# Seven products instead of eight in part of the first MLP, and a new order behind the attention

## The chip, the cores and the metric

The kernel runs as one program on one core of a Trainium2 chip. The core has five engines that take their instructions in order, each from its own queue: TensorE (PE in the profile, with its weight loads shown apart as PEld), VectorE (DVE), ScalarE (ACT), GpSimd (POOL) and SyncE (SP, which here only issues DMAs). They wait for each other through semaphores. The metric is the device time of one execution in microseconds, as the median over runs. Before the change it is 654.48 us (three runs, 653.82 to 654.96).

## The reference

Three stages, each feeding the next, in float32:

```
out_d     = attention of q, k, v averaged over groups of 4 positions, repeated 4 times
out_local = attention within |i - j| < 4
x   = (out_d + out_local), as 1152 tokens x 512                 # 2 batches of 576
h   = x @ w_in                                                  # 512 -> 2048
x   = where(h > 0, h, exp(min(h, 0)) - 1) @ w_out              # 2048 -> 512, "first MLP"
for e in 4 experts:                                             # "second MLP"
    out += p[:, e] * (relu(x @ w1[e]) @ w2[e])                  # 512 -> 1024 -> 512
```

`p` is `domain_probs` with its rows normalized. `w_in` and `w_out` come as 64-bit floats, of which the kernel makes 32-bit ones itself.

## The kernel before

**Number form.** TensorE works on a 32-bit type with a shorter mantissa. Every operand X is therefore split into a high part (a copy into that type, on ACT) and a low part (X minus the high part, on DVE or POOL), and every product is three matmuls: high x high, low x high, high x low (`PASSES`, `mm3`, L237 to L242). All matmuls that the change touches have a 128x128 stationary operand and 288 moving columns.

**Stages.** The attention of batch 0 and 1 runs first (`Attn`). The first MLP cuts its 2048 features into four quarters s = 0 to 3 of 512 and the 1152 tokens into four blocks t = 0 to 3 of 288 (t = 0, 1 are batch 0, t = 2, 3 batch 1). In a quarter, f = 0 to 3 counts blocks of 128 features, mt = 0 to 3 blocks of 128 output columns. The second MLP (from L1023) runs over eight pieces of 512 features; in it the first product already stands in seven-product form (`quad`, L1075), and its first piece, n = 0, uses weights prepared during the first MLP.

**Steps.** The work up to the second MLP is one long string `ORDER` (L23), read from left to right; a step is named by its letters and its indices, and ":v" or ":g" puts it on DVE or POOL. Each engine runs its own steps in the order of this string. The steps that matter here:

- `hp.s.t.f` (PE, L788): x times one block of `w_in`, four stretches of 128 inputs, so 12 matmuls into one of eight PSUM banks. `yp.s.t.mt` (PE, L829): features times `w_out`, again 12 matmuls.
- `ha`, `he` (ACT), `hd` (DVE): the activation; `hh` (ACT) and `hl` (DVE or POOL): high and low part `g` of its result; `ya` (DVE, for s = 0 ACT): adds the bank of `yp` to the accumulator.
- `wF` (DMA), `wA` (ACT), `wB` to `wE` (DVE, L274, L280, L287, L294), `wH` (ACT) and `wL` (DVE or POOL, L308): fetch of a 64-bit weight piece, conversion to 32 bits, high and low part.
- `xh`, `xl`, `xd`, `xth`, `xtl`: high and low parts, and differences, of the accumulators, as inputs of the second MLP's first product.
- `mF`, `mS`, `mH`, `mL`, `nF`, `nH`, `nL`: weights of piece n = 0 of the second MLP: fetch, sums (POOL, L348), high parts (ACT), low parts (POOL, L376, L400).
- `C`: the attention's memory is given up, and pools that take its place are opened (L931 to L937).

Behind `C` stand 41 `hp` and 46 `yp`. Tiles live in slots (`Slots`, L121): one that is given back goes to the end of a list, and the next tile waits, through semaphores, for the last reader of the tile before it in its slot. In the second MLP the same kind of steps is started from a list of due times (`due`, `plan`, L1293 to L1348); after the first MLP, `xd` and then `first_xt` (L1336) for the second half of the tokens come from there, on POOL.

## Time and profile before

| | us |
|---|---|
| median of 3 runs | 654.48 |
| the profiled execution's own time | 654.35 |
| its span, first to last instruction | 652.6 |
| PE busy | 645.2 |
| DVE / ACT / POOL busy | 450.7 / 302.2 / 316.9 |
| behind `C` up to the second MLP, 139.31 to 277.91 us: length | 138.60 |
| there: PE / DVE / ACT / POOL busy | 138.60 / 96.70 / 80.66 / 53.94 |

The span is what the profiler saw of the core; 1.75 us of the execution lie around it. Busy times are unions of an engine's instructions, so instructions that overlap are counted once, and an instruction held up after its start by something that the profile doesn't show as a wait is still counted as busy. A wait is shown as idle time ahead of an instruction, with what ended it.

### The profile page before, as it was taken

Reading aid. Unit: us, or ns where it says so; the run is one execution under the profiler, and the core shown is the slowest. Engines: PE = TensorE matmul, PEld = TensorE weight load, DVE = VectorE, ACT = ScalarE, POOL = GpSimd, SP = SyncE. Lnnn points to the kernel's source line nnn. Section 1 sums busy time; section 2 is a strip of 40 time slices with the busy share of each in tenths; the row PEclk is TensorE's granted clock in tenths of the full one; section 3 lists DMA queues with packets and bytes.
Section 4 is the critical chain, followed back from the end, with each engine's and each line's share of the span. In section 5 each row is a group of like instructions: output and inputs, shape, how many; then the busy total and the mean of one; then the engine's idle time right before and its main releaser. Section 6 shows DMA issues by size and latency. Waiting matters only on the chain.

```text
span 652.6 us, 12355 instructions
## 1 busy us (share of the span) xinstructions
PE 645.2 (99%) x4804; PEld 593.0 (91%) x4804; DVE 450.7 (69%) x957; ACT 302.2 (46%) x825; POOL 316.9 (49%) x312
## 2 busy tenths in 40 slices
...
GB/s 240 211 200 224 166 87 11 1 196 66 65 130 65 130 2 1 2 65 1 66 65 1 112 18 7 124 0 66 66 2 64 66 1 67 62 1 66 1 48 97
DMA packets 40880, 46.70 MB, mean 72 GB/s; under 512 B 23030, under 2 KB 23286, under 8 KB 40822
## 3 DMA queue, kind: packets, MB, share of 16 engines
...
q14 instruction: 20, 0.16, 0.1%
...
## 4 chain that ended last, share of the span: by engine, by line
PE 91%; DVE 4%; DMA 3%; issue 1%; ACT 0%; SPq 0%; DVEq 0%
PE psZ L240 30%; PE psH L240 17%; PE psY L240 14%; PE psE L240 7%; PE psA L240 6%; PE psG L240 3%; PE psF L240 3%; PE psB L240 2%; PE psS L585 1%; PE psX L645 1%; DMA raw<-in_k_dram 1%; DMA raw<-in_moe_w_in_dram 1%; PE psP L629 1%; PE psC L240 1%; PE psGT L736 1%; PE psG L682 1%
## 5 line engine op out<-in xcount | busy, mean ns | idle before, releaser
L240 PE MATMUL psZ<-wr,h 128*128 128x512 f32 (+2 forms) x876 | 226.8, 390 | 0.0
L240 PEld LDWEIGHTS psZ<-wr,h 128*128 128x128 f32 x876 | 154.4, 188 | 22.1
L240 PE MATMUL psH<-x,w 128*128 128x288 f32 x768 | 108.0, 296 | 1.7 <-DVE w L308 1.4
L240 PE MATMUL psY<-g,w 128*128 128x288 f32 x768 | 106.3, 296 | 0.1
L240 PEld LDWEIGHTS psH<-x,w 128*128 128x128 f32 x768 | 103.3, 188 | 3.3 <-DVE w L308 2.2
L240 PEld LDWEIGHTS psY<-g,w 128*128 128x128 f32 x768 | 103.3, 188 | 0.5 <-DVE g L826 0.3
L1138 DVE SCALAR_TENSOR_TENSOR oacc<-psZ,pn,oacc 128x512 f32<-128x512 f32 (+1 forms) x64 | 47.4, 740 | 45.1 <-PE psZ L240 45.1
L1043 ACT ACTIVATE h<-psF 128x288 fp32r<-128x288 f32 x28 | 11.5, 412 | 118.2 <-DVE psF L1037 118.2
L826 POOL TENSOR_TENSOR g<-gf,g 128x288 fp32r<-128x288 f32 x25 | 22.0, 883 | 80.6 <-ACT g L821 78.0
L240 PEld LDWEIGHTS psE<-xt,ws 128*128 128x128 f32 x336 | 48.6, 188 | 3.3
L240 PE MATMUL psE<-xt,ws 128*128 128x288 f32 x336 | 50.6, 295 | 0.0
L1000 POOL TENSOR_TENSOR wq<-raw,wq 128x512 fp32r<-128x512 f32 x21 | 27.0, 1301 | 47.1 <-ACT wq L996 42.9
L400 POOL TENSOR_TENSOR wr<-raw,wr 128x1024 fp32r<-128x1024 f32 x16 | 38.6, 2419 | 21.0 <-ACT wr L395 20.9
L1037 DVE TENSOR_TENSOR c<-psE,c 128x288 f32<-128x288 f32 x56 | 25.4, 456 | 33.7 <-PE psE L240 33.4
L1010 POOL TENSOR_TENSOR raw<-raw 128x256 f32<-128x256 f32 x56 | 42.6, 766 | 3.4
L821 ACT ACTIVATE g<-gf 128x288 fp32r<-128x288 f32 x64 | 27.3, 440 | 28.2 <-DVE gf L814 21.3
L814 DVE SCALAR_TENSOR_TENSOR gf<-m,psH 128x288 f32<-128x288 f32 x64 | 28.0, 446 | 16.7 <-ACT m L809 11.9
L1037 DVE TENSOR_TENSOR c<-psA,c 128x288 f32<-128x288 f32 x62 | 26.6, 454 | 17.8 <-PE psA L240 16.6
L395 ACT ACTIVATE wr<-raw 128x1024 fp32r<-128x1024 f32 x16 | 16.8, 1058 | 43.1 <-DMA raw<-in_moe_w_dram 22.7
L1018 POOL TENSOR_TENSOR ws<-raw,ws 128x1024 fp32r<-128x1024 f32 x14 | 34.1, 2457 | 2.5 <-ACT ws L1014 2.5
L805 ACT ACTIVATE m<-psH 128x288 f32<-128x288 f32 x64 | 25.3, 402 | 19.4 <-PE psH L240 14.9
L308 POOL TENSOR_TENSOR w<-raw,w 128x512 fp32r<-128x512 f32 x12 | 18.6, 1550 | 30.2 <-ACT w L303 30.2
...
## 6 DMA issues: line engine op xcount, KB each, us to landing
...
```

The costliest lines, as they stand in the source:

```text
L240: nc.tensor.matmul(ps, wt[a], xt[b], start=first and n == 0, stop=last and n == 2, skip_group_check=more)
L308: ENG[eng].tensor_tensor(out=t[:, 1, r], in0=up.bitcast(F32), in1=t[:, 0, r].bitcast(F32), op=ALU.subtract)
L400: nc.gpsimd.tensor_tensor(out=t[:, 1], in0=raw[0][:, 2 * j:2 * j + 2], in1=t[:, 0].bitcast(F32), op=ALU.subtract)
L805: nc.scalar.activation(m, ps1["h", s, t, f][:, :HB], AF.Relu, scale=-1.0)
L814: nc.vector.scalar_tensor_tensor(out=gf, in0=m, scalar=-1.0, in1=ps[:, :HB], op0=ALU.add, op1=ALU.max)
L821: nc.scalar.activation(g[:, 0], ps1["gf", s, t, f], AF.Copy)
L826: ENG[eng].tensor_tensor(out=g[:, 1], in0=gf, in1=g[:, 0].bitcast(F32), op=ALU.subtract)
L1000: tt(out=lo, in0=x, in1=hi.bitcast(F32), op=sub)
L1010: tt(out=o, in0=a, in1=b, op=op)
L1018: tt(out=w[:, 1], in0=raw[0][:, :, 2 * j * P:2 * (j + 1) * P], in1=w[:, 0].bitcast(F32), op=sub)
L1037: nc.vector.tensor_tensor(out=o, in0=y, in1=x, op=add_)
L1138: nc.vector.scalar_tensor_tensor(out=a, in0=ps, scalar=sc, in1=a, op0=ALU.mult, op1=ALU.add)
```

## The change

For the last quarter (s = 3), the four `hp` steps that share a pair of feature blocks (j = 0 or 1) and a batch (b = 0 or 1) form a 2x2 block product, over two halves of the inputs: eight block products, each 2x3 matmuls. In three of the four such groups (`QUADS`) they are replaced by seven products `qp.s.j.b.k`, of sums and differences of the blocks. The fourth group, (3, 1, 1), keeps its four `hp`. For this:

- `xa` (eight steps a batch, DVE or POOL, 128x576) forms four sums of x, `xi` (ACT) and `xj` (DVE or POOL) their high and low parts. They live in new tiles, for batch 0 in memory that is given back at a new step `D`.
- `vS` (four steps a j, DVE) forms sums of the converted weights in place, `vH` (ACT) and `vL` (DVE or POOL) their high and low parts, in two new tiles.
- `qc` (three steps a group, ACT) copies one PSUM bank at three points, and `qd` (five steps a group, DVE) adds the pieces; products 3 and 6 accumulate into the bank of product 0.
- The pool of three large tiles becomes three pools of one.
- All of `ORDER` behind `C` is written anew: 533 steps before, 615 now. Steps common to both stand in another order and partly on another engine. Up to `C` nothing differs.

```diff
 ORDER = """
...
-1LPh.6 ha.1.2.3 1LPl.6:v yp.0.2.0 C wF.2.1:b ya.0.2.0 ya.0.2.1 hh.1.2.0 wF.2.0:b wA.2.0 he.1.2.3 wA.2.1 hl.1.2.0:v
...
+1LPh.6 ha.1.2.3 1LPl.6:v yp.0.2.0 C hp.0.3.2 ya.1.1.3 he.1.2.3 wF.2.0:b xa.0.0:g wF.2.1:b hh.1.2.0 ya.1.0.2 hh.1.2.1
...
-    xp = ctx.enter_context(tc.tile_pool(name="xp", bufs=3))
+    xp = [ctx.enter_context(tc.tile_pool(name=f"xp{i}", bufs=1)) for i in range(3)]
...
+        def quarters(p):
+            a, b = (piece(2 * p + i)[2].bitcast(F32) for i in range(2))
+            return a[:, :, :P], a[:, :, P:], b[:, :, :P], b[:, :, P:]
+        def vS(p, o, eng="g"):
+            f0a, f1a, f0b, f1b = quarters(p)
+            out, x, y, op = (
+                (f1b, f1a, f1b, ALU.add), (f1a, f0a, f1a, ALU.subtract), (f0a, f1b, f0a, ALU.subtract),
+                (f0b, f0b, f0a, ALU.subtract),
+            )[o]
+            ENG[eng].tensor_tensor(out=out, in0=x, in1=y, op=op)
+        def vH(p, i):
+            shape, r, up, _ = piece(2 * p + i)
+            if i == 0:
+                wv[p] = s8.tile([P, 2, *shape], F32R, name="v64", uses=sums[p])
+            nc.scalar.activation(wv[p][:, 0, r], up.bitcast(F32), AF.Copy)
+        def vL(p, i, eng="g"):
+            _, r, up, _ = piece(2 * p + i)
+            ENG[eng].tensor_tensor(
+                out=wv[p][:, 1, r], in0=up.bitcast(F32), in1=wv[p][:, 0, r].bitcast(F32), op=ALU.subtract
+            )
+            where[p].done(raw[p])
...
+        QUADS = {(3, 0, 0), (3, 1, 0), (3, 0, 1)}
+        def quads(s, j):
+            return sum((s, j, b) in QUADS for b in range(2))
...
+        def xa(b, k, eng="g"):
+            if k == 0:
+                xs[b] = (xp[2] if b else bo[0]).tile([P, 4, 2, 2, HB], F32R, tag="x" if b else "xs", name="xs")
+                x32[b] = bo[1].tile([P, 4, 2, HB], F32, tag="x32", name="x32")
+            o = [x32[b][:, n] for n in range(4)]
+            def x(h, i):
+                return [xb[b][:, m, 2 * h:2 * h + 2, i * HB:(i + 1) * HB].bitcast(F32) for m in range(2)]
+            out, x, y, op = (
+                (o[0], *x(0, 0), ALU.add), (o[1], *x(0, 1), ALU.add), (o[0], o[1], o[0], ALU.subtract),
+                (o[2], *x(1, 1), ALU.add), (o[1], o[2], o[1], ALU.subtract), (o[2], o[2], o[0], ALU.subtract),
+                (o[3], *x(1, 0), ALU.add), (o[3], o[3], o[2], ALU.subtract),
+            )[k]
+            ENG[eng].tensor_tensor(out=out, in0=x, in1=y, op=op)
+        def xi(b, n):
+            nc.scalar.activation(xs[b][:, n, 0], x32[b][:, n], AF.Copy)
+        def xj(b, n, eng="g"):
+            x = xs[b][:, n]
+            ENG[eng].tensor_tensor(out=x[:, 1], in0=x32[b][:, n], in1=x[:, 0].bitcast(F32), op=ALU.subtract)
+        def qp(s, j, b, k):
+            w, v = wt[s][0][j], wv[s][j]
+            def wb(w, h, i):
+                return [w[:, m, 2 * h:2 * h + 2, i * P:(i + 1) * P] for m in range(2)]
+            def xv(h, i):
+                return [xb[b][:, m, 2 * h:2 * h + 2, i * HB:(i + 1) * HB] for m in range(2)]
+            def xn(n):
+                return [xs[b][:, n, m] for m in range(2)]
+            (wh, wl), (h, l) = (
+                lambda: (wb(w, 0, 0), xv(0, 0)), lambda: (wb(w, 1, 0), xv(1, 0)), lambda: (wb(v, 1, 1), xn(0)),
+                lambda: (wb(v, 0, 0), xn(2)), lambda: (wb(v, 1, 0), xv(1, 1)), lambda: (wb(w, 1, 1), xn(3)),
+                lambda: (wb(v, 0, 1), xn(1)),
+            )[k]()
+            if k == 0:
+                if not ct:
+                    c = st_pool[0].tile([P, 4, 2, P], F32, tag="st", name="ct").rearrange("p a b c -> p (a b c)")
+                    ct.extend(c[:, i * HB:(i + 1) * HB] for i in range(3))
+                ps1["q", s, j, b] = [ct]
+            q = ps1["q", s, j, b]
+            if k in (3, 6):
+                q.append(None)
+            else:
+                q.append(bank("psQ"))
+            ps = q[1 if k in (3, 6) else k + 1][:, :HB]
+            for kk in range(2):
+                mm3(ps, (wh[:, kk], wl[:, kk]), (h[:, kk], l[:, kk]), k not in (3, 6) and kk == 0, kk == 1, k in (3, 6))
+            if k == 5:
+                s8.done(w)
+            if k == 6:
+                s8.done(v)
+        def qc(s, j, b, n):
+            q = ps1["q", s, j, b]
+            nc.scalar.activation(q[0][n], q[1][:, :HB], AF.Copy)
+            if n == 2:
+                psb_.done(q[1])
+        def qd(s, j, b, n):
+            q = ps1["q", s, j, b]
+            c1, u2, u3 = q[0]
+            ps = q[(2, 3, 5, 6, 3)[n]]
+            y = ps[:, :HB]
+            nc.vector.tensor_tensor(
+                out=u2 if n == 1 else y, in0=y, in1=(c1, u2, u2, u3, u3)[n], op=ALU.add
+            )
+            if n != 1:
+                i, k = {0: (0, 0), 2: (0, 1), 3: (1, 0), 4: (1, 1)}[n]
+                ps1["h", s, 2 * b + k, 2 * j + i] = ps
...
-                xto[pair] = xp.tile([P, 4, 2, 2, HB], F32R, tag="x", name="xt")
+                xto[pair] = xp[1 - pair].tile([P, 4, 2, 2, HB], F32R, tag="x", name="xt")
...
+                bo.extend(xst.enter_context(tc.tile_pool(name=x, bufs=1)) for x in ("xs", "x32"))
...
+            if tok == "D":
+                xst.close()
+                bo[:] = [ctx.enter_context(tc.tile_pool(name="bo", bufs=2))]
+                continue
...
-        oacc = xp.tile([P, NTT, DM], F32, tag="x", name="oacc")
+        oacc = xp[2].tile([P, NTT, DM], F32, tag="x", name="oacc")```

**VectorE just behind `C`.** `g` is a low part (`hl`), `acc` an accumulation (`ya`), `gf` the activation (`hd`), `xf` the attention's last work, `cv` and `raw` the conversion of weights. Before:

```order
227 L656 TENSOR_TENSOR xf<-psX,od 128x256
228 L670 TENSOR_TENSOR x_831<-xf,x_831 128x4x64
229 L826 TENSOR_TENSOR g<-gf,g 128x288
230 L274 TENSOR_SCALAR cv<-cv 128x512
231 L280 TENSOR_SCALAR cv<-cv 128x512
232 L274 TENSOR_SCALAR cv<-cv 128x512
233 L287 SCALAR_TENSOR_TENSOR raw_2624<-raw_2624,cv 128x512
```

Now, where the 128x576 rows are `xa` and the last row is the low part `hl.1.2.2`, which the ninth PE step behind `C` (`yp.1.2.0`) reads:

```order
232 L855 TENSOR_TENSOR x_2644<-x_326 128x576
233 L941 TENSOR_TENSOR g<-gf,g 128x288
234 L929 SCALAR_TENSOR_TENSOR gf<-m,psH 128x288 x2
235 L941 TENSOR_TENSOR g<-gf,g 128x288
236 L855 TENSOR_TENSOR x_2644<-x_326 128x576
237 L855 TENSOR_TENSOR x_2644<-x_2644 128x576 x2
238 L929 SCALAR_TENSOR_TENSOR gf<-m,psH 128x288
239 L281 TENSOR_SCALAR cv<-cv 128x512 x2
240 L287 TENSOR_SCALAR cv<-cv 128x512 x2
241 L294 SCALAR_TENSOR_TENSOR raw_2641<-raw_2641,cv 128x512 x2
242 L301 SCALAR_TENSOR_TENSOR raw_2641<-raw_2641 128x512 x2
243 L941 TENSOR_TENSOR g<-gf,g 128x288
```

The weight conversion moved behind the activations and four new sums, and one low part, on POOL before, stands behind all of it.

**TensorE in the last quarter.** `psQ` are the products of the new form, `x_326` and `x_837` the two batches, `xs` their sums, `v` the sums of weights:

```order
296 L247 MATMUL psQ<-x_326,w_3405 128x288 x12
297 L247 MATMUL psQ<-xs,v_3470 128x288 x12
298 L247 MATMUL psQ<-x_326,v_3470 128x288 x6
299 L247 MATMUL psQ<-xs,w_3405 128x288 x6
300 L247 MATMUL psQ<-xs,v_3470 128x288 x6
```

This is one group: seven products in 42 matmuls where four `hp` had 48. There are three such groups, and 18 matmuls fewer.

**POOL at the passage to the second MLP.** `ws` and `wr` are low parts of weights of piece n = 0, `st` sums of them, `xbo` and the first `xt` rows low parts of the first half, `acc` and the last `xt` row the second half (`xd`, `first_xt`). Before:

```order
82 L376 TENSOR_TENSOR ws<-st,ws 128x4x256
83 L826 TENSOR_TENSOR g<-gf,g 128x288 x2
84 L871 TENSOR_TENSOR xbo<-acc,xbo 128x288 x2
85 L826 TENSOR_TENSOR g<-gf,g 128x288
86 L890 TENSOR_TENSOR xt<-acc,xt 128x576
87 L871 TENSOR_TENSOR xbo<-acc,xbo 128x288
88 L880 TENSOR_TENSOR acc<-acc 128x576 x3
89 L890 TENSOR_TENSOR xt<-acc,xt 128x576 x4
```

Now:

```order
94 L380 TENSOR_TENSOR st<-raw_3936,st 128x256
95 L986 TENSOR_TENSOR xbo<-acc,xbo 128x288
96 L408 TENSOR_TENSOR ws<-st,ws 128x4x256
97 L432 TENSOR_TENSOR wr<-raw_4054,wr 128x1024
98 L995 TENSOR_TENSOR acc<-acc 128x576 x3
99 L1005 TENSOR_TENSOR xt<-acc,xt 128x576 x4
```

The last `ws` and `wr` moved to the very end, between the last low part of the first MLP and the differences that the second MLP's third group reads.

## Rows read from the trace of the kernel before

**Rows 1.** The page's busy times: us, share of the span, instructions.
```profile
PE 645.2 (99%) x4804; PEld 593.0 (91%) x4804; DVE 450.7 (69%) x957; ACT 302.2 (46%) x825; POOL 316.9 (49%) x312
```

**Rows 2.** Windows: length; PE, PEld, DVE, ACT, POOL busy; clock; DMA; GB/s.
```profile
40.00:80.00 40.00, 38.58 (x452) 35.55 (x448) 39.58 (x76) 33.61 (x108) 19.11 (x18) 1.00 0.99 208
80.00:120.00 40.00, 39.19 (x415) 37.29 (x414) 37.10 (x86) 30.89 (x116) 12.51 (x14) 1.00 0.16 43
200.00:240.00 40.00, 40.00 (x304) 40.00 (x304) 32.95 (x56) 20.86 (x49) 16.73 (x16) 1.00 0.23 80
139.31:277.91 138.60, 138.60 (x1046) 138.60 (x1045) 96.70 (x188) 80.66 (x189) 53.94 (x50) 1.00 0.18 62
```

**Rows 3.** Timeline of TensorE: start, us, line, out<-in, count.
```profile
139.31 3.35 PE L240 MATMUL psH<-x,w 128*128 128x288 f32 x24
...
277.91 1.76 PE L240 MATMUL psH<-xbo,wa 128*128 128x288 f32 x12
...
289.11 1.76 PE L240 MATMUL psH<-xbo,wa 128*128 128x288 f32 x12
...
293.91 0.96 PE L240 MATMUL psH<-xt,ws 128*128 128x288 f32 x6
```

**Rows 4.** VectorE groups, 160 to 278 us: xcount | busy us, mean ns | idle.
```profile
L854 DVE TENSOR_TENSOR acc<-psY,acc 128x288 f32<-128x288 f32 x36 | 15.4, 449 | 10.1 <-PE psY L240 10.1
L826 DVE TENSOR_TENSOR g<-gf,g 128x288 fp32r<-128x288 f32 x20 | 12.9, 648 | 2.8 <-ACT g L821 2.7
L294 DVE SCALAR_TENSOR_TENSOR raw<-raw 128x512 uint32<-128x512 uint32 x12 | 9.6, 796 | 0.2
...
L274 DVE TENSOR_SCALAR cv<-cv 128x512 f32<-128x512 f32 x12 | 7.6, 636 | 6.7 <-ACT cv L270 6.7
...
L880 DVE TENSOR_TENSOR acc<-acc 128x576 f32<-128x576 f32 x4 | 3.0, 750 | 0.0
```

**Rows 5.** Timeline of VectorE, single instructions.
```profile
137.35 0.42 DVE L670 TENSOR_TENSOR x<-xf,x 128x256 fp32r<-128x256 f32 x1 [0.48 <-ACT x L665]
...
141.72 0.43 DVE L280 TENSOR_SCALAR cv<-cv 128x512 uint32<-128x512 uint32 x1
...
144.29 0.69 DVE L294 SCALAR_TENSOR_TENSOR raw<-raw 128x512 uint32<-128x512 uint32 x1
...
275.36 0.75 DVE L890 TENSOR_TENSOR xt<-acc,xt 128x576 fp32r<-128x576 f32 x1
...
279.44 1.36 DVE L890 TENSOR_TENSOR xt<-acc,xt 128x576 fp32r<-128x576 f32 x1
```

**Rows 6.** Timeline of GpSimd at the passage to the second MLP.
```profile
279.08 1.11 POOL L871 TENSOR_TENSOR xbo<-acc,xbo 128x288 fp32r<-128x288 f32 x1
281.92 4.47 POOL L880 TENSOR_TENSOR acc<-acc 128x576 f32<-128x576 f32 x3 [1.73 <-DVE acc L880]
...
287.97 4.22 POOL L890 TENSOR_TENSOR xt<-acc,xt 128x576 fp32r<-128x576 f32 x3 [0.19 <-ACT xt L886]
```

**Rows 7.** GpSimd groups, 160 to 278 us.
```profile
L826 POOL TENSOR_TENSOR g<-gf,g 128x288 fp32r<-128x288 f32 x18 | 16.0, 890 | 42.2 <-ACT g L821 42.2
L308 POOL TENSOR_TENSOR w<-raw,w 128x512 fp32r<-128x512 f32 x7 | 10.6, 1511 | 20.4 <-ACT w L303 20.4
L376 POOL TENSOR_TENSOR ws<-st,ws 128x1024 fp32r<-128x1024 f32 x2 | 4.8, 2407 | 3.2 <-ACT ws L370 3.2
L400 POOL TENSOR_TENSOR wr<-raw,wr 128x1024 fp32r<-128x1024 f32 x2 | 4.8, 2400 | 0.0
```

**Rows 8.** Timeline of ScalarE, one instruction.
```profile
288.08 0.69 ACT L886 ACTIVATE xt<-acc 128x576 fp32r<-128x576 f32 x1
```

More of the change, by code (lines that the diff above doesn't have):

```diff
@@ L112 @@
-xth.0.2 xd.0.3 xth.0.3 yp.3.3.2 yp.3.3.1 xtl.0.3:g xtl.0.2:v xl.2.2:v xth.0.1 ya.3.3.1 yp.3.3.3 ya.3.3.2 ya.3.3.3
-xh.3.2 xh.3.3 xl.3.2:v xtl.0.1:v xl.2.3:g xl.3.3:v
+1LPh.6 ha.1.2.3 1LPl.6:v yp.0.2.0 C hp.0.3.2 ya.1.1.3 he.1.2.3 wF.2.0:b xa.0.0:g wF.2.1:b hh.1.2.0 ya.1.0.2 hh.1.2.1
+ya.0.2.0 ya.0.2.1 hl.1.2.1:v hp.1.2.2 hl.1.2.0:g ha.0.3.2 hd.1.2.3 hh.1.2.3 xa.0.1:v he.0.3.2 yp.0.2.2 hl.1.2.3:v
+ha.1.2.2 hd.0.3.2 xa.0.2:g he.1.2.2 hh.0.3.2 hd.1.2.2 hp.0.3.0 ya.0.2.2 hl.0.3.2:v xa.0.3:v hp.0.3.1 xa.0.4:v
@@ new lines @@
+he.2.1.1 hl.2.0.0:v hh.2.1.0 xa.1.1:g hp.2.1.2 hd.2.0.1 ha.2.0.2 hh.2.0.1 he.2.0.2 hl.2.0.1:v hp.2.0.3 hl.2.1.0:g
+hd.2.0.2 hh.2.0.2 wC.2.4 ha.2.1.2 hl.2.0.2:v hp.2.1.3 he.2.1.2 wB.2.5 wD.2.4 wC.2.5 yp.1.3.0 wE.2.4 wA.3.0 wD.2.5
+wH.2.4 hd.2.1.2 xa.1.2:g yp.1.3.1 hd.2.1.1 ha.2.0.3 ya.1.3.0 ha.2.1.3 he.2.0.3 wE.2.5 he.2.1.3 yp.1.3.2 wA.3.1
+wL.2.4:v wH.2.5 ya.1.3.1 xa.1.3:g yp.1.3.3 ya.1.3.2 wL.2.5:v wB.3.0 wF.3.1:b hp.2.2.0 wB.3.1 hh.2.1.2 ya.1.3.3
+xa.1.4:g hh.2.1.1 hp.2.3.0 hl.2.1.2:v xi.1.1 hl.2.1.1:g hd.2.0.3 hh.2.0.3 hp.2.2.1 xa.1.5:g hd.2.1.3 ha.2.2.0
@@ new lines @@
+xh.1.3 hl.3.2.2:v hp.3.3.3 xl.1.3:v ha.3.3.2 xd.0.0 he.3.3.2 mL.0.0 xth.0.0 hd.3.3.2 yp.3.2.0 ha.3.3.3 hh.3.3.2
+xd.0.1 he.3.3.3 mH.0.2 yp.3.2.1 hl.3.3.2:g hd.3.3.3 ya.3.2.0 xd.0.2 hh.3.3.3 xth.0.1 yp.3.2.2 hl.3.3.3:v ya.3.2.1
+mL.0.2 xth.0.2 xh.2.1 yp.3.2.3 xh.2.0 ya.3.2.2 xh.2.2 xd.0.3 yp.3.3.0 ya.3.2.3 mS.1.0 xth.0.3 xtl.0.0:v xh.2.3
+yp.3.3.1 ya.3.3.0 mS.1.1 xtl.0.3:v yp.3.3.2 mS.1.2 ya.3.3.1 xtl.0.2:v yp.3.3.3 xtl.0.1:v ya.3.3.2 mS.1.3 xh.3.2
+xl.2.0:v mH.1.2 ya.3.3.3 xl.3.2:g xl.2.1:v xh.3.3 xl.2.3:v nH.0 xl.3.3:v xl.2.2:v mL.1.2 nL.0
@@ L244, in attn_moe_kernel, with fetch64, weights64 @@
     pools = [s8]
-    def fetch64(w, shape, pool):
-        raw = pool.tile([P, *shape, 2], U32, name="raw64", uses=2)
+    def fetch64(w, shape, pool, uses=2):
+        raw = pool.tile([P, *shape, 2], U32, name="raw64", uses=uses)
         nc.sync.dma_start(raw.rearrange("p n m w -> p n (m w)"), w)
         return raw
-    def weights64(parts, cv):
+    def weights64(parts, cv, sums=(), wv=None):
         raw, where, tmp = {}, {}, {}
```

105 lines of the change are left out of this document (55 added, 50 removed).

## The prediction

> **What bounds the kernel now.** I read the busy times first. TensorE is busy for 99% of the span, no other engine for more than 69% [rows 1]. That alone doesn't say that fewer matmuls give a shorter time, so I read the windows next, for the stage that is rewritten, from `C` at 139.31 us, where the first product behind it starts, to 277.91 us, where the second MLP's first product starts [rows 3]. There TensorE is busy for all of 138.60 us, at the full granted clock, and DVE for 96.70, ACT for 80.66, POOL for 53.94 [rows 2]. So today this stage is as long as its matmuls, and the three other engines have 30%, 42% and 61% of it free. Two more windows tell what happens where DVE is fuller: from 200 to 240 us it is busy for 32.95 of 40 us (82%) and TensorE loses nothing; from 80 to 120 us, in the attention, 37.10 of 40 (93%), and TensorE has lost 0.81 us; from 40 to 80 us 39.58 of 40, and TensorE has lost 1.42 [rows 2]. The question is on which of these stretches the new stage is modelled.
>
> **What is removed.** The stage has 41 `hp` and 46 `yp` of 12 matmuls, 1,044 in all, in 138.60 us: 0.1328 us each. Three groups lose one product of 6 matmuls, 18 in all: 18 x 0.1328 = 2.39 us. TensorE pays that in full today, so with no new wait the time falls from the profiled execution's own 654.35 us (span 652.6 and 1.75 around it; the median is 654.48, 0.13 more) to 651.96. This is all that can be won: the stage has no idle time of TensorE that a better order could remove.
>
> **What is added on DVE.** Prices are those of instructions that nothing held up. Four `xa` and three `xj` at 0.75 [rows 4, 5]: 5.25 us. Fifteen `qd` at 0.449, the price of an addition that reads a PSUM bank [rows 4]: 6.74. Eight `vS` of 256 elements at 0.42 [rows 5]: 3.36. Three `vL`, and two `wL` that come over from POOL, at 0.69, the price of a 512-element instruction with two inputs [rows 5]: 3.45. One `hl` and two `xl` at 0.45 (between 0.42 for 256 elements and 0.449) and one `xtl` at 0.75: 2.1. Sum 20.9 us. 96.70 + 20.9 = 117.6 us in a stage of 138.60 - 2.39 = 136.21: 86%.
>
> **What is added on POOL and ACT.** POOL: twelve `xa` at 4.47 / 3 = 1.49 and five `xj` at 4.22 / 3 = 1.41 [rows 6] are 24.9; one `vL` more and two `wL` less at 1.51, three low parts of 288 elements at 0.89 [rows 7] and one `xtl` at 1.41 less are -5.6. So 53.94 + 19.3 = 73.2 us, of which three instructions of 0.89 + 2.41 + 2.40 = 5.7 us [rows 7] now fall behind the end of the stage: 67.5 within it. ACT: 21 instructions (eight `xi`, four `vH`, nine `qc`), none larger than the 128x576 copy of 0.69 us [rows 8]: at most 14.5, so at most 95.2 of 136.2. ACT and POOL have room enough; DVE is the engine to watch.
>
> **DVE held up by POOL.** The durations above are those of a free DVE. At 279.44 a 576-element low part took 1.36 us instead of 0.75 [rows 5], while POOL worked at 279.08 to 280.19 [rows 6]: it ended 0.61 us after POOL did. In the groups the same shows as means: 0.648 for 0.45, 0.796 for 0.69, 0.636 for 0.43, while additions that read PSUM stay at 0.449 [rows 4, 5]. Over the 44 instructions of those three groups that is 4.0 + 1.3 + 2.5 = 7.8 us on 22.4, or 35%. The 96.70 already hold this for the old work. The new and moved work that reads SBUF alone is 14.2 us, so 35% of it is 5.0; and POOL goes from 39% to 50% of the stage, so what is held up today (35% of about 74 us of such work, 26 us) may grow by a quarter, 7 us. DVE then has 117.6 to 129.6 us of work, 86% to 95%.
>
> The Trainium skill, in "SBUF — State Buffer", section "Who interferes with whom", says that a DVE instruction with two SBUF inputs and a GpSimd instruction that reads SBUF exclude each other, and that the later one waits for the whole of the earlier. The 1.36 us agree with that. By this rule what counts is not 86% but the sum of both engines' work on SBUF, which is the second rival below.
>
> **Three places where a wait can come up.** First, behind `C`. The low part `hl.1.2.2` stood on POOL and now ends a row of DVE work. Ahead of it stands the activation of the product `hp.0.3.0`, TensorE's fourth step, which ends at 139.31 + 4 x 12 x 0.1328 = 145.69. Two ACT steps (at most 0.69 each) and one DVE step (0.449) later it is 147.5; then four instructions at 0.43, four at 0.69 and the low part, 4.9 us: 152.4. TensorE's ninth step starts at 139.31 + 8 x 1.594 = 152.06 and reads this block of features after 6 matmuls, at 152.86. That leaves 0.4 us, and one POOL instruction of 1.41 (`xj.0.0`) falls into the row. Bounds: 0 and 1.0 us lost; I take 0.3, nearer to 0, since both ACT steps are priced at their bound.
>
> Second, the passage to the second MLP. POOL's last low part of the accumulators, the `ws` and the `wr` take 5.7 us. If they start with the end of the last `yp`, POOL reaches the three differences 5.7 us behind it (today 281.92 - 277.91 = 4.0), ends them at 10.2 and the four low parts (4 x 1.41) at 15.8. The product that reads the last of these starts at 293.91, 16.0 behind [rows 3]. The margin is 0.2, before 1.7. DVE's own tail decides whether POOL starts on time. Bounds: 0 and 1.2 lost (one 576-element instruction of DVE held up, and its reader); I take 0.3.
>
> Third, the rest of the stage, some 120 us, in which DVE runs at 86% or more. Bounds: 0, as at 82%, and 120 x 2.0% = 2.4, as at 93%. Most of what TensorE reads there was finished long before, counted in DVE's order, so I stay near the lower row: 0.3. Where DVE is late, PSUM banks are what is missing next: a group holds five banks of eight where four `hp` held four, and the additions `ya` and `qd` that free them queue behind the sums.
>
> **Sum.** -2.39 + 0.3 + 0.3 + 0.3 = -1.5: 654.35 - 1.5 = 652.85, or 652.9. All unknowns at their lower ends give 651.96, all at their upper ends (1.0 + 1.2 + 2.4) 656.56. The likeliest case by itself: 651.8 to 653.2.
>
> **Rivals.** *No change, as DVE is too full to answer at once.* DVE runs at 90% to 93% and TensorE loses as it did at 80 to 120 us: 2.0% of 136.21 is 2.7 us, which pays back the whole gain: 651.96 + 2.7 = 654.7 (653.2 to 655.8). For it: 129.6 us is 95%. Against it: that stretch had shorter matmuls and the attention's chains, and 82% costs nothing.
>
> *Slower: DVE and POOL fill what they share.* DVE's work on SBUF alone is then 32 conversions at 0.43 (13.8), 32 at 0.69 (22.1), 12 low parts of weights at 0.69 (8.3), 34 of 288 elements at 0.45 (15.3), eight sums at 0.42 (3.4) and fifteen instructions at 0.75 (11.3): 74.2 us. With POOL's 67.5 that is 141.7. DVE is free from 137.77 on (its last work of the attention, 137.35 + 0.42 [rows 5]), 1.5 us ahead of the stage, so the stage would last 140.2 instead of 138.60: 654.35 + 1.6 = 655.9. With the 35% on top of the 74.2 and 99 instructions that read PSUM at 0.449 (44.5) DVE alone needs 144.7: 143.2 for the stage, 658.9. In the middle 657. It decides from the point where DVE has under 5% of the stage idle. For it: the 1.36 us, and 59 us of both engines in the 40 us from 40 to 80, where TensorE lost most. Against it: the measured means say that most instructions meet no POOL instruction, the same sum for the old stage (60 + 53.9 of 138.6) left TensorE whole, and instructions that follow each other closely overlap a little.
>
> *The change doesn't do what it says* would show as 654.4; the order of instructions excludes it, with 18 matmuls fewer.
>
> **Chances.** Forecast 0.48, no change 0.26, slower 0.26. A measurement of this kernel can tell 0.2%, 1.3 us, from no change: faster means below 653.2. The forecast lies almost wholly there, the first rival within the bound, the second above it: 0.48, 0.26, 0.26. The range for 8 in 10 goes from 651.4 (0.5 below the full gain, as runs of one kernel differ) to 657.0, the middle of the slower case.
>
> **What would show it.** In the profile after: TensorE with 18 matmuls fewer in the stage, the stage 136 to 137.5 us long, DVE at 85% to 92% of it, idle time of TensorE of under 1 us in all, ended by DVE's low parts about 13 us behind `C` and by POOL's `xt` in the second MLP's third group. It is wrong if TensorE's idle time in the stage passes 2 us, if the idle time is ended by PSUM banks or by `v` and `xs` (then the new form's own preparation is late), or if DVE has no idle time left, which would be the slower case. Behind the third group the second MLP should be unchanged.

## The result, and the profile after

| | before | after |
|---|---|---|
| median, us (runs) | 654.72 (4) | 660.55 (4) |
| lowest to highest, us | 653.82 to 655.35 | 659.34 to 662.5 |
| ratio, 95% interval | | 1.0093 [1.0065, 1.0121] |
| stage behind `C`, us, profiled execution | 138.60 | 142.71 |
| from the second MLP's first product to the end, us | 374.7 | 376.7 |

The change makes the kernel 0.9% slower; the forecast was 652.9 us, with 651.4 to 657.0 as the range. The profiled execution after is the slowest of the four, 662.5 us. Busy times of the page, after (compare [rows 1]):

```profile
PE 645.7 (98%) x4786; PEld 592.3 (90%) x4786; DVE 484.6 (73%) x996; ACT 311.2 (47%) x846; POOL 338.2 (51%) x324
```

The 18 matmuls are gone (4804 to 4786), yet TensorE is no less busy. The window of the stage and four of 1 us inside it (columns as in [rows 2]):

```profile
141.30:284.01 142.71, 138.66 (x1029) 137.73 (x1028) 125.41 (x225) 87.46 (x208) 70.36 (x60) 0.99 0.18 63
223.00:224.00 1.00, 0.37 (x1) 0.37 (x2) 0.69 (x2) 1.00 (x4) 0.51 (x1) 0.69 0.02 8
224.00:225.00 1.00, 1.00 (x6) 1.00 (x6) 1.00 (x3) 1.00 (x3) 0.00 (x0) 0.50 0.00 0
225.00:226.00 1.00, 1.00 (x6) 1.00 (x6) 1.00 (x3) 1.00 (x4) 0.00 (x0) 0.50 0.00 0
226.00:227.00 1.00, 1.00 (x6) 1.00 (x6) 0.96 (x2) 1.00 (x3) 0.67 (x1) 0.60 0.00 0
```

TensorE now idles 4.05 us of a stage in which it never idled, and about 1.5 us of its busy time are matmuls at half clock: from 224 us on one starts every 0.24 us instead of every 0.13, with 0.50 granted. Its waits in the stage and the first 16 us behind it (engine, tile, line <- releaser: us in total, times, longest):

```profile
PE psQ L247 <- ACT ct L902: 2.8, 1, 2.8
PE psH L247 <- ACT c L1166: 1.0, 1, 1.0
PE psY L247 <- DVE g L941: 1.0, 1, 1.0
PE psH L247 <- DVE gf L929: 0.2, 1, 0.2
```

For the whole account I take the time from each matmul's start to the next one's start and add up what lies beyond 0.1328 us. This gives 1.23 us lost at 13.7 us behind `C`, 0.49 and 0.37 at 50.6 and 63.8, 4.44 in the first group of the new form (2.9 of waiting, 1.5 of half clock). That is 6.53 - 2.39 = +4.14 for the stage (measured 142.71 - 138.60 = +4.11). In the second MLP 1.29 at 8.0 us behind its start and some 0.7 at 17, so +2.0. Together 6.1, of which the medians show 5.8. (`C` itself came 2.0 us later in this profile; among the profiles below, with the same work ahead of `C`, it came at 138.2 to 141.8 us, so nothing is read from that.)

The large wait, engine by engine (timelines, columns as in [rows 3]; POOL, DVE, ACT, PE):

```profile
214.79 1.88 POOL L855 TENSOR_TENSOR x<-x 128x576 f32<-128x576 f32 x1
218.35 1.31 POOL L315 TENSOR_TENSOR w<-raw,w 128x512 fp32r<-128x512 f32 x1 [1.67 <-ACT w L310]
219.62 1.64 POOL L855 TENSOR_TENSOR x<-x 128x576 f32<-128x576 f32 x1
...
213.67 0.41 DVE L287 TENSOR_SCALAR cv<-cv 128x512 uint32<-128x512 uint32 x1
...
215.31 1.65 DVE L287 TENSOR_SCALAR cv<-cv 128x512 uint32<-128x512 uint32 x1
...
218.64 1.34 DVE L941 TENSOR_TENSOR g<-gf,g 128x288 fp32r<-128x288 f32 x1 [0.71 <-ACT g L936]
219.90 1.90 DVE L294 SCALAR_TENSOR_TENSOR raw<-raw,cv 128x512 uint32<-128x512 uint32 x1
221.73 0.81 DVE L929 SCALAR_TENSOR_TENSOR gf<-m,psH 128x288 f32<-128x288 f32 x2
...
222.20 0.44 ACT L936 ACTIVATE g<-gf 128x288 fp32r<-128x288 f32 x1 [1.63 <-DVE gf L929]
...
223.17 0.40 ACT L902 ACTIVATE ct<-psQ 128x288 f32<-128x288 f32 x1
...
223.63 1.81 PE L247 MATMUL psQ<-xs,v 128*128 128x288 f32 x6 [2.77 <-ACT ct L902]
```

Read it from below. TensorE waits for `qc` (`ct`), which stands on ACT behind a copy `hh` that waits 1.63 us for DVE's `hd` (L929). The `hd` is late because the instructions ahead of it took 1.65, 1.34 and 1.90 us, where 0.41, 0.45 and 0.69 are the free prices, and each ends 0.3 to 0.5 us behind a POOL instruction: the sum `xa` that started at 214.79 ends at 216.67, DVE's at 216.96; the one from 219.62 ends at 221.26, DVE's at 221.80. The middle one stands beside a low part of weights (L315), not a sum. By this reading a wait shown as one for ACT is a wait for POOL, three engines back, and no view names POOL in it.

The place behind `C` (DVE, then POOL, then PE):

```profile
151.51 2.53 DVE L294 SCALAR_TENSOR_TENSOR raw<-raw,cv 128x512 uint32<-128x512 uint32 x2
153.96 1.28 DVE L301 SCALAR_TENSOR_TENSOR raw<-raw 128x512 uint32<-128x512 uint32 x2
155.16 1.05 DVE L941 TENSOR_TENSOR g<-gf,g 128x288 fp32r<-128x288 f32 x1
...
151.45 1.44 POOL L862 TENSOR_TENSOR xs<-x,xs 128x576 fp32r<-128x576 f32 x1 [4.83 <-ACT xs L858]
155.10 0.80 POOL L941 TENSOR_TENSOR g<-gf,g 128x288 fp32r<-128x288 f32 x1 [2.22 <-ACT g L936]
...
156.26 2.01 PE L247 MATMUL psY<-g,w 128*128 128x288 f32 x13 [0.96 <-DVE g L941]
```

It is the place and the row of instructions that the prediction named; POOL's `xj` falls into it and adds 1.2 us to the first two. The last of the row, the low part that TensorE waits for, took 1.05 us for 0.45 beside a low part on POOL. That these two made it late is read from this timeline; no run takes them out alone.

The passage to the second MLP (POOL, DVE, ACT, PE; the POOL rows answer to [rows 6]):

```profile
284.70 2.60 POOL L408 TENSOR_TENSOR ws<-st,ws 128x1024 fp32r<-128x1024 f32 x1
287.26 2.61 POOL L432 TENSOR_TENSOR wr<-raw,wr 128x1024 fp32r<-128x1024 f32 x1
291.31 4.43 POOL L995 TENSOR_TENSOR acc<-acc 128x576 f32<-128x576 f32 x3 [1.43 <-DVE acc L995]
295.69 5.62 POOL L1005 TENSOR_TENSOR xt<-acc,xt 128x576 fp32r<-128x576 f32 x4
...
284.58 5.98 DVE L986 TENSOR_TENSOR xbo<-acc,xbo 128x288 fp32r<-128x288 f32 x4
290.48 0.75 DVE L995 TENSOR_TENSOR acc<-acc 128x576 f32<-128x576 f32 x1
...
291.26 0.69 ACT L1001 ACTIVATE xt<-acc 128x576 fp32r<-128x576 f32 x1 [3.30 <-DVE acc L995]
291.85 0.39 ACT L1166 ACTIVATE c<-psH 128x288 f32<-128x288 f32 x1
301.35 0.41 ACT L1169 ACTIVATE h<-psH 128x288 fp32r<-128x288 f32 x1 [2.61 <-POOL xt L1005]
...
293.32 1.07 PE L247 MATMUL psH<-xt,ws 128*128 128x288 f32 x6 [1.02 <-ACT c L1166]
```

Four low parts that cost 0.45 each take 5.98 us on DVE, beside POOL's `ws` and `wr`. So `xd` is late, ACT's `xth` behind it, and the copy `c` behind that, for which TensorE waits. The kernel order_alone below, which has the new order without the new form, shows the same 5.98 us (DVE there):

```profile
279.01 5.98 DVE L978 TENSOR_TENSOR xbo<-acc,xbo 128x288 fp32r<-128x288 f32 x4
```

POOL's chain, late by as much, ends at 301.31, and ACT's `h` at 301.35 waits for it: the last 0.7 us.

### The profile page after: what moved, and what is told of

It reads as the page before. It is cut to its first block, busy times and chain, and to the rows that moved or that the text cites. A ratio compares the mean times of both kernels' runs of the same rounds, so it can differ in the third digit from the quotient of the medians.

```text
span 660.7 us, 12385 instructions
## 1 busy us (share of the span) xinstructions
PE 645.7 (98%) x4786; PEld 592.3 (90%) x4786; DVE 484.6 (73%) x996; ACT 311.2 (47%) x846; POOL 338.2 (51%) x324
## 4 chain that ended last, share of the span: by engine, by line
PE 75%; DVE 13%; DMA 4%; ACT 3%; issue 2%; POOL 1%; SPq 1%; DVEq 0%; ACTq 0%
PE psZ L247 30%; PE psY L247 9%; PE psE L247 7%; PE psH L247 6%; PE psA L247 6%; DMA raw<-in_moe_w_in_dram 4%; PE psG L247 3%; PE psF L247 3%; PE psQ L247 2%; DVE raw L294 2%; PE psB L247 2%; DVE g L941 2%; DVE w L315 1%; DVE raw L301 1%; PE psX L677 1%
## 5 line engine op out<-in xcount | busy, mean ns | idle before, releaser
L247 PE MATMUL psZ<-wr,h 128*128 128x512 f32 (+2 forms) x876 | 226.8, 390 | 0.0
L247 PEld LDWEIGHTS psZ<-wr,h 128*128 128x128 f32 x876 | 154.4, 188 | 22.1
L247 PE MATMUL psY<-g,w 128*128 128x288 f32 x768 | 105.6, 296 | 1.2 <-DVE g L941 1.0
L247 PEld LDWEIGHTS psY<-g,w 128*128 128x128 f32 x768 | 103.0, 188 | 2.1 <-DVE g L941 1.5
L247 PE MATMUL psH<-x,w 128*128 128x288 f32 x624 | 87.7, 297 | 1.9 <-DVE w L315 1.4
L247 PEld LDWEIGHTS psH<-x,w 128*128 128x128 f32 x624 | 83.7, 188 | 3.7 <-DVE w L315 2.1
L1169 ACT ACTIVATE h<-psF 128x288 fp32r<-128x288 f32 x28 | 11.5, 412 | 118.3 <-DVE psF L1163 118.3
L247 PEld LDWEIGHTS psE<-xt,ws 128*128 128x128 f32 x336 | 48.6, 188 | 3.3
L247 PE MATMUL psE<-xt,ws 128*128 128x288 f32 x336 | 50.6, 295 | 0.0
L432 POOL TENSOR_TENSOR wr<-raw,wr 128x1024 fp32r<-128x1024 f32 x16 | 38.8, 2429 | 21.4 <-ACT wr L427 21.4
L941 POOL TENSOR_TENSOR g<-gf,g 128x288 fp32r<-128x288 f32 x24 | 20.7, 866 | 53.3 <-ACT g L936 44.0
L936 ACT ACTIVATE g<-gf 128x288 fp32r<-128x288 f32 x64 | 27.3, 440 | 22.4 <-DVE gf L929 17.3
L941 DVE TENSOR_TENSOR g<-gf,g 128x288 fp32r<-128x288 f32 x40 | 29.8, 752 | 8.7 <-ACT g L936 8.4
L1126 POOL TENSOR_TENSOR wq<-st,wq 128x512 fp32r<-128x512 f32 x18 | 23.1, 1300 | 20.0 <-ACT wq L1122 20.0
L315 POOL TENSOR_TENSOR w<-raw,w 128x512 fp32r<-128x512 f32 x10 | 14.5, 1454 | 29.4 <-ACT w L310 29.4
```

Source lines behind the costliest of these rows:

```text
L247: nc.tensor.matmul(ps, wt[a], xt[b], start=first and n == 0, stop=last and n == 2, skip_group_check=more)
L315: ENG[eng].tensor_tensor(out=t[:, 1, r], in0=up.bitcast(F32), in1=t[:, 0, r].bitcast(F32), op=ALU.subtract)
L432: nc.gpsimd.tensor_tensor(out=t[:, 1], in0=raw[0][:, 2 * j:2 * j + 2], in1=t[:, 0].bitcast(F32), op=ALU.subtract)
L936: nc.scalar.activation(g[:, 0], ps1["gf", s, t, f], AF.Copy)
L941: ENG[eng].tensor_tensor(out=g[:, 1], in0=gf, in1=g[:, 0].bitcast(F32), op=ALU.subtract)
L1126: tt(out=lo, in0=x, in1=hi.bitcast(F32), op=sub)
```

## The experiments

**Theory.** An instruction of POOL that reads SBUF holds an instruction of DVE with inputs in SBUF until it ends; the 12 sums `xa` on POOL do this at places where TensorE's chain bears no delay. **Rivals.** ACT's queue order; DVE's sum of work, whoever else runs; POOL being busy, whatever it does; the new order of the steps.

Stage and "rest" (from the second MLP's first product on) are those of one profile each; before they are 138.60 and 374.7. Each ratio is to runs of the kernel before from the same round, whose median was 654.17 to 654.75.

| kernel | median us | ratio [95%] | stage | rest |
|---|---|---|---|---|
| no_xa | 655.10 | 1.0013 [1.0003, 1.0023] | 137.38 | 376.7 |
| qc_early | 661.07 | 1.0100 [1.0085, 1.0115] | 141.89 | 376.7 |
| xa_later | 659.54 | 1.0075 [1.0060, 1.0090] | 141.32 | 376.7 |
| order_alone | 656.26 | 1.0025 [1.0007, 1.0043] | 138.44 | 376.6 |
| pool_xa_out | 655.55 | 1.0026 [1.0014, 1.0038] | 137.38 | 376.7 |
| xa_fill | 655.14 | 1.0022 [1.0008, 1.0035] | 137.38 | 377.0 |
| xa_dve | 655.50 | 1.0018 [1.0006, 1.0030] | 137.48 | 376.7 |
| fixes | 663.81 | 1.0149 [1.0131, 1.0168] | 142.06 | 379.6 |
| two_fixed | 657.41 | 1.0055 [1.0035, 1.0075] | 136.96 | 379.8 |
| passage2 | 660.09 | 1.0085 [1.0064, 1.0105] | 142.00 | 376.5 |
| order_passage2 | 655.18 | 1.0014 [1.0001, 1.0026] | 138.44 | 375.5 |
| two_v2 | 654.67 | 1.0003 [0.9992, 1.0014] | 136.96 | 376.5 |
| three_dve | 653.18 | 0.9988 [0.9977, 1.0000] | 136.31 | 376.5 |
| three_dve_p3 | 654.30 | 1.0001 [0.9990, 1.0012] | 136.28 | 376.4 |
| order_passage3 | 655.39 | 1.0019 [1.0007, 1.0030] | 138.44 | 376.0 |
| three_dve_p4 | 654.95 | 1.0010 [0.9996, 1.0024] | 136.22 | 377.2 |
| order_passage4 | 658.06 | 1.0056 [1.0040, 1.0072] | 138.44 | 378.1 |
| three_dve_p5 | 656.55 | 1.0030 [1.0016, 1.0043] | 136.18 | 378.3 |

Line numbers in these kernels differ from the changed kernel's by a few.

**no_xa**: all 16 sums left out; the splits read x itself.

```diff
-            nc.scalar.activation(xs[b][:, n, 0], x32[b][:, n], AF.Copy)
+            nc.scalar.activation(xs[b][:, n, 0], xsum(b, n), AF.Copy)   # a view of x itself
```

> The changed kernel without its 16 sums of x (xa): the high and low parts xi and xj are taken of one block of x itself, so the products of the new form get other numbers, in the same count and shape. Theory 1 (DVE is late because POOL's and its own xa hold up its work on SBUF): the waits of 1.1 us behind C and of 2.9 us in the first group go, and with the second the 1.5 us at half clock; what is left is the passage (1.3 us): 654.4 - 2.4 + 1.4 = about 653.5, DVE under 118 us busy in the stage. Rival (the chain of the new form itself: copy of the bank, ACT's order): the wait of 2.9 us stays, time 658 or more.

The groups' waits are gone, and with them some 5 us. A miss for the wait behind `C`: theory 1 expected it to go, and it stays at 1.2 us, so the sums don't make it; the 2.0 us of the passage stay too.

**qc_early**: one step moved on ACT.

```diff
-qp.3.0.0.0 hh.2.3.2 hd.2.2.3 ... hh.2.2.3 qc.3.0.0.0
+qp.3.0.0.0 qc.3.0.0.0 hh.2.3.2 hd.2.2.3 ... hh.2.2.3
```

> One step moved: the first copy of a bank in group (3,0,0) (qc.3.0.0.0) goes ahead of two high parts and an activation on ACT. Nothing is lighter. If ACT's order alone made the wait of 2.9 us, it goes with its 1.5 us of half clock: about 656. Theory 1 (DVE is behind as a whole): the wait comes back at the next thing that DVE owes, a bank or a low part, in part: 657.5 to 660.5.

The wait moved to the next `qc` of the same group (2.06 us, ahead of its seventh product) and the time stayed, 0.6 us above what theory 1 had as its upper end. So the place of this one step is not the cause; xa_dve below, with ACT's order as in the changed kernel, takes ACT's order out as a whole.

**xa_later**: `xa.1.6`, `xa.1.7`, `xi.1.3` behind the first group's last product.

> Two sums of batch 1 on POOL (xa.1.6, xa.1.7) and one high part move behind the first group (3,0,0), which doesn't read them. Theory 1: DVE's conversions at this place take 0.41 and 0.69 us again instead of 1.65 and 1.90, the wait of 2.9 us and the 1.5 us of half clock go: about 656. Rival (DVE has too much work whoever else runs, or the chain of the new form): the wait stays, 659 or more.

A miss for theory 1: the time is the rival's, 659 or more. The 4.44 us fall to 1.30 and the clock stays up, but 1.7 us come back as four smaller waits further on. Two of these, at 102 and 107 us behind `C`, stand where qc_early loses 0.4 and 0.6 us, and the second where passage2 loses 0.6, with the two sums where they were. No sum of POOL runs there, so DVE seems late there from before. A hold-up moved is not a hold-up removed.

**order_alone**: the new order, plain products in all groups, nothing of the new form.

> The new order with the four plain products in all four groups of the last quarter; xa, xi, xj, vS, vH, vL, qc, qd gone, so 18 matmuls and the waits of the new form's load are both away. Theory 1: the waits behind C and in the first group go, the passage's 1.3 us stay: 654.5 + 1.4 = about 656, DVE at some 100 us in the stage. Rival (the new order itself is worse): 658 or more.

As expected: TensorE idle for 0.0 us in the stage, all of the loss (2.0) in the second MLP. The order in itself costs the passage, nothing else.

**pool_xa_out and xa_fill** tell hold-ups from load. The first leaves out the 12 sums on POOL (what would read them reads x itself or DVE's sums), the second writes zeros in their place. Both edits in one, other lines left out:

```diff
+            if eng == "g":
+                return                                   # pool_xa_out
+                for o in (out, out, out[:, 0]):          # xa_fill, in place of the return
+                    nc.gpsimd.memset(o, 0.0)
             ENG[eng].tensor_tensor(out=out, in0=x, in1=y, op=op)
```

> Left out: the 12 of the 16 sums of x that GpSimd forms (those of the second half's 8, and 4 of the first half's); the split reads x itself in their place. VectorE keeps its own 4 sums, and all else stays. Theory 1 (GpSimd's reads of SBUF hold VectorE's two-input instructions up, and these hold-ups make VectorE late): the 2.9 us wait of TensorE in the first group, the half clock behind it and the other waits of that stretch go, what is lost behind C (1.2) and at the passage (1.3) stays: 655 to 656. Rival (VectorE has too much to do, whoever else runs): its instructions stay as many, so the waits stay too: 658 to 660.5.

> The 12 sums of x on GpSimd are replaced by memsets into the same tile, two and a half for each, which by the rows of the three memsets in the first microseconds (128x128 f32 took 204 ns, 128x1 took 98) come to an estimated 1.4 us: GpSimd is as busy as with the sums, but reads nothing there; the sums' values are lost. Theory 1, in its narrower form (it is GpSimd's reading that holds up VectorE, not its being busy): as with the 12 sums left out, 655 to 656.5. Rival (GpSimd is too full, or any of its work holds VectorE up): 659 to 661.

The window of the stage in pool_xa_out, with two DVE groups there:

```profile
139.61:277.00 137.39, 136.43 (x1029) 136.20 (x1028) 113.60 (x225) 88.18 (x207) 52.88 (x49) 1.00 0.19 65
...
L952 DVE TENSOR_TENSOR g<-gf,g 128x288 fp32r<-128x288 f32 x25 | 16.1, 654 | 7.2 <-ACT g L947 7.1
...
L287 DVE TENSOR_SCALAR cv<-cv 128x512 uint32<-128x512 uint32 x16 | 6.3, 419 | 0.0
```

The same groups in the changed kernel, and its sums on POOL:

```profile
L941 DVE TENSOR_TENSOR g<-gf,g 128x288 fp32r<-128x288 f32 x25 | 20.4, 824 | 6.4 <-ACT g L936 6.2
...
L287 DVE TENSOR_SCALAR cv<-cv 128x512 uint32<-128x512 uint32 x16 | 9.4, 613 | 0.0
...
L855 POOL TENSOR_TENSOR x<-x 128x576 f32<-128x576 f32 x11 | 17.8, 1625 | 1.8 <-DVE x L855 1.6
```

And xa_fill:

```profile
141.84:279.22 137.38, 136.42 (x1028) 136.19 (x1027) 114.73 (x225) 88.27 (x207) 69.71 (x82) 1.00 0.20 65
...
L857 POOL MEMSET x<- 128x576 f32 (+1 forms) x33 | 17.4, 535 | 1.3
```

DVE runs the same 225 instructions in all three: 125.41 us beside the sums, 113.60 without them, 114.73 beside memsets that keep POOL as busy (69.71 for 70.36 us) but read nothing. So 11.8 us of DVE's "busy" time was waiting for POOL, about 1 us for each sum, and it is POOL's reading that does it. The Trainium skill, in "SBUF — State Buffer", section "Who interferes with whom", says just this: a DVE instruction with two SBUF inputs contends with GpSimd instructions that read SBUF and not with those that only write; the 113.60 and 114.73 us agree. It also names `tensor_scalar` among the operations that can, under conditions, run in a two-port mode and then contend, which agrees with L287, one input and 613 ns for 419.

**xa_dve**: the sums stay and change their engine.

```diff
-xa.0.0:g xa.0.2:g xa.0.6:g ... xa.1.7:g
+xa.0.0:v xa.0.2:v xa.0.6:v ... xa.1.7:v
```

> The changed kernel with one thing changed: its 12 sums of x on GpSimd are done by VectorE, at the same places of the order; nothing left out. Theory 1 (what cost the time is that a GpSimd instruction that reads SBUF holds a VectorE instruction for its whole length, at places where TensorE's chain bears no delay): the waits of the groups go, what is lost behind C (1.2) and at the passage (2.0) stays: 654.5 to 656. Rival (VectorE's sum of work, 9 us more now): 659 or more.

5 us won by giving DVE 9 us more of work. The rival of the sum of work falls, and so does ACT's order, which is unchanged here. The only wait of TensorE left in the stage is the one behind `C`:

```profile
PE psY L246 <- DVE g L940: 1.0, 1, 1.0
```

With the two other fixes in **three_dve** (`hh.1.2.2`, `hl.1.2.2` ahead of the two `wE`; `nH.0`, `nL.0` earlier, `xl.2.1 xl.2.2` ahead of the last `ya`, `xl.3.3` on POOL):

> Nothing left out: three groups, the early move and the passage's moves, and all 16 sums of x on VectorE. VectorE takes on 12 x 0.75 = 9 us of work of its own; GpSimd reads 18 us less, and with its 12 sums gone VectorE's same 225 instructions took 113.6 us in place of 125.4. So VectorE's busy time comes to 122 to 123 us, hardly less than with the hold-ups. Theory 1 (what made TensorE wait is that single instructions were held for a whole GpSimd instruction, at places where the chain could not bear it): most waits go, 652 to 654.5. Rival (it is the sum of VectorE's busy time that counts, held up or not): 657 to 659.

The stage is 136.31 us: all 2.3 us of the matmuls won, no wait of TensorE left in it. The window of the stage, xa_dve's:

```profile
138.24:275.72 137.48, 136.51 (x1028) 136.18 (x1027) 121.31 (x236) 87.97 (x207) 54.21 (x49) 1.00 0.19 65
```

and three_dve's:

```profile
139.91:276.22 136.31, 136.31 (x1028) 136.18 (x1027) 119.33 (x234) 88.36 (x206) 57.06 (x49) 1.00 0.18 63
```

DVE is busy for 119.33 / 136.31 = 88% and TensorE loses nothing; in the changed kernel it is 125.41 / 142.71 = 88% too, and TensorE loses 6.5 us.

**The place behind `C` and the passage.** In **fixes** `hl.1.2.2` goes ahead of DVE's two `wE` (and, unlike the words below, stays behind both `wD`), and the passage is put otherwise (`mL.1.2` ahead of the last `xl`); **two_fixed** is that with two groups.

> Nothing left out; six steps moved: hl.1.2.2 ahead of the two wE and the second wD on VectorE, hh.1.2.2 with it; the last two weight splits of the second MLP (nH.0, nL.0) to some 12 us earlier, the split of its sums (mH.1.2, mL.1.2) ahead of the last xl on GpSimd, and xl.2.0 and xl.2.1 some 6 us earlier on VectorE. Theory 1: the 1.2 us behind C and the 1.3 us at the passage go and nothing else changes: 657.5 to 658.5. Rival (VectorE is late as a whole, so that what is won at one place is lost at the next): 659.5 to 661.

> The same moves, and two groups instead of three: the group of the second half of the rows goes back to plain products, and its 8 sums of x on GpSimd, 4 copies on ScalarE and 4 splits go with it. 12 matmuls are saved in place of 18 (1.6 us by 0.1328). Theory 1: with GpSimd's 8 sums gone in the stretch where VectorE was held up, 653 to 654.3. Rival (VectorE too full by the corrections themselves): the waits in the two groups stay, 655 to 657.5.

The 1.23 us behind `C` are gone in both, though in fixes some 0.5 us of it come back at 49 us behind `C`, where the wait for `hd` is 0.7 us instead of 0.2. Both times missed their range, since the passage got worse: in fixes POOL's `ws` now stands beside two `xtl` of DVE (3.39 us), the last two `ya` queue behind them, ACT's `xh` and `c` behind those, and TensorE waits 3.52 us. So it went in the other arrangements too: `ya` behind `xl` in two_v2 and order_passage2 (1.6 and 0.6 us), `xd` behind `xl` in three_dve_p3 and order_passage3 (1.2 and 0.8). All four came out above the range that the theory gave:

> Nothing left out: two groups instead of three (no sums of x for the second half, so 8 of GpSimd's 12 sums go), the early move of hl.1.2.2 and hh.1.2.2, and the moves at the passage of this batch in place of those of the kernel with six moves. Theory: the stage as in that one (136.96 us in its profile, TensorE without a wait), the stretch behind at about 374.7 us: before less 12 x 0.1328 = 1.6 us, 652.4 to 653.4, faster than the kernel before. Rival (the passage's wait comes back at another instruction): 654.5 to 656.5.

> The new order with plain products in all groups, as in order_alone, with the passage put otherwise: nH.0 and nL.0 some 20 us earlier, xl.2.1 and xl.2.2 ahead of the last acc sum on VectorE, xl.3.3 on GpSimd, mL.1.2 behind it as GpSimd's last split. Theory: all that the new order costs is the passage (1.3 us of wait there, 0.7 us further on, through GpSimd's late xt splits): the stretch from the start of the second MLP goes from 376.6 back to about 374.7 us, and the time to 654 to 655, as before. Rival (the order costs elsewhere too): 656.

> As three_dve, with the passage put once more: the split xtl.0.1, three of the xl of the second half and the copy c's forerunner mH.1.2 in such places that VectorE does the last two acc sums before them and ScalarE reaches its first copy c without waiting for VectorE. Nothing left out. Theory (the 1.6 us at the passage are ScalarE's copy c queued behind xh.3.3, which waits for the last acc sum, itself queued behind splits on VectorE): the stretch from the start of the second MLP on goes from 376.45 to 374.7 to 375.3 us, the time to 651.3 to 652.3, faster than before. Rival (VectorE is behind at the passage in any order): 653 or more.

> As order_passage2 (the new order, plain products in all groups), with the passage of three_dve_p3. Theory: the 0.9 us that stood there against the kernel before (375.54 against 374.66) go: 654 to 654.6, as before. Rival (the new order costs at the passage wherever its splits stand): 655 to 656.

In three_dve_p3, DVE, POOL and ACT:

```profile
278.21 3.02 DVE L985 TENSOR_TENSOR xbo<-acc,xbo 128x288 fp32r<-128x288 f32 x2
...
277.63 2.92 POOL L407 TENSOR_TENSOR ws<-st,ws 128x1024 fp32r<-128x1024 f32 x1
...
281.93 0.69 ACT L1000 ACTIVATE xt<-acc 128x576 fp32r<-128x576 f32 x1 [3.19 <-DVE acc L994]
```

Then POOL's late work was taken away from there, by putting `nL.0` on DVE in the second MLP (three_dve_p4; order_passage4 is the same with plain products), and by doing `mS.1` and `mL.1.2` some 10 us earlier as well (three_dve_p5):

> As three_dve_p3, nothing left out, with the passage arranged so that no GpSimd instruction of 1.2 us or more stands beside VectorE's last splits: mL.1.2 goes ahead of the xl on GpSimd, three xl go from VectorE to GpSimd behind it, and the last weight split of the second MLP (nL.0) is done by VectorE some 10 us into the second MLP, nH.0 with it. Theory (the passage's 1.2 us are xd.1.0 on VectorE behind two xl that GpSimd's split ws holds for 3.02 us in three_dve_p3): the stretch from the start of the second MLP goes from 376.40 to 374.7 to 375.3 us, with the stage at 136.3; against before 0.995 to 0.998. Rival (what is moved off the passage comes back behind it, where xt and wr are waited for): 376 us or more, ratio 0.999 to 1.001.

> Three groups, all sums of x on VectorE, the early move, nothing left out; the weights of the second MLP in another order: the first split of sums (mL.0.2) some 13 us earlier, the sums mS.1 and their split mL.1.2 behind it in the 10 us in which VectorE and GpSimd stood half idle (255 to 265 us in three_dve_p3), the split nL.1 behind these, nH.0 and nL.0 (on VectorE) in the second MLP. Theory (the passage's 2 us are GpSimd's late work: what it splits last holds VectorE's last splits, or if put behind them, ends too late): with that work done earlier the stretch from the start of the second MLP takes 374.7 to 375.3 us and the stage 136.2 to 136.6: against before 0.995 to 0.998, faster. Rival (VectorE, ScalarE or the second MLP itself are late there for another reason): 376 us or more, 0.999 to 1.001; or the earlier splits hold VectorE up in the stage: stage over 137.5.

Both missed, and so did order_passage4, for which 0.999 to 1.000 had been expected. In three_dve_p5 what is lost at 3 and 8 us behind the second MLP's start falls to 0.2 and 0 us, as the theory has it, but a wait of 1.85 comes up at 12.8, and behind it some 1.7 us of half clock (0.50 granted from 292 to 295 us): `nL.0` stands beside POOL's `xt` and takes 2.43 us, ACT's next `wq` starts 0.1 us behind its end, and a copy `c` is queued behind that (DVE, POOL, ACT):

```profile
286.59 2.43 DVE L431 TENSOR_TENSOR wr<-raw,wr 128x1024 fp32r<-128x1024 f32 x1
...
285.12 6.69 POOL L1004 TENSOR_TENSOR xt<-acc,xt 128x576 fp32r<-128x576 f32 x4
...
289.11 0.63 ACT L1121 ACTIVATE wq<-raw 128x512 fp32r<-128x512 f32 x1 [2.40 <-issue]
```

The view names no releaser for that `wq`; in three_dve_p4 it names this `nL.0`. There `nL.0` started 0.1 us ahead of POOL's `xt` (287.11 and 287.20) and took 1.22 us. The late `nL.0` is a fault of this edit, so whether the new order can have a passage without loss stays open: 0.9 us (375.5 against 374.7, order_passage2) is the least seen. passage2 (three groups, sums on POOL, passage as in two_v2) won 0.2 us in the rest, and nothing that its interval shows; 658 to 659 had been expected.

No version is shown to be faster than the kernel before. three_dve comes nearest, 0.9988 with 1.0000 as the interval's end; three_dve_p3, with a shorter profile, gave 1.0001.

## Why the prediction was wrong

- **The gain** was right: 17 matmuls fewer in the stage's records and 18 in all, and 2.3 of the 2.39 us appear as soon as nothing waits (three_dve).
- **DVE's and POOL's work** was sized rightly: 117.6 to 129.6 predicted, 125.41 measured; 67.5, and 70.36 measured, in part because a sum took 1.625 us for 1.49. DVE is at 88%, within the 85% to 92% announced.
- **The step that failed** is the third place, "the rest of the stage": 0.3 us, with 0 to 2.4 as bounds, taken from two stretches by DVE's busy share. It was 5.3 us (0.49 + 0.37 + 4.44). The busy share doesn't decide it: 88% costs nothing in three_dve and 6.5 us after the change. What decides is which instruction is held, for how long, and what queues behind it. The 35% of hold-up was averaged over the stage (12 us at most in all; 11.8 are what the sums' hold-ups measured), while it comes in portions of 0.9 to 1.3 us, three of them close together ahead of one `hd`. "Finished long before" doesn't hold inside a group: the fourth product adds to the bank of the first, which `qc` must have copied, and on ACT this `qc` stands behind steps that wait for DVE. That path had no term. I expected PSUM banks to run out there; a bank was what TensorE waited for, but through ACT and DVE, and xa_dve, with the same path, doesn't wait.
- **Behind `C`**: place, row and the POOL instruction that falls into it were named; 0.3 taken, 1.23 measured, above the bound of 1.0. The `xj` was seen and not added to the 4.9 us.
- **The passage**: 0.3 taken with 1.2 as bound, 2.0 measured. I priced POOL's chain by POOL alone. DVE's four `xl` beside `ws` and `wr` (5.98 us for 1.8) made it start late; "DVE's own tail decides" stood there without a price.
- **A cost without a term**: about 1.5 us of half clock behind a wait, in the profiled execution.
- **The rival "slower"** had the exclusion of the two engines right and the wrong point from which it decides: DVE under 5% idle. It had 12% idle (17.3 of 142.7 us). Its stage of 140.2 to 143.2 us holds the measured 142.71, but by luck, since DVE never filled it; and its 657 was too low, as it had no term for the 2.0 us of the passage.

What is shown: the sums' reads on POOL as the cause of the stage's waits behind the one at `C`, the 0.49 and 0.37 us among them (gone in no_xa, pool_xa_out, xa_fill, xa_dve and three_dve); that the early move takes away the wait behind `C`; and the order's price at the passage (order_alone). Argued from single timelines only: which instructions of POOL make the wait behind `C` and the one at the passage.
